# Attention with a mixture of experts on one core: sum rounds gathered, q's turn and the proposals moved within the attention steps

## The chip, the core and the metric

The kernel runs on one core of a Trainium2 chip. The time is that of one execution on the device in microseconds (us); a kernel's time is the median of several executions. The engines are TensorE (PE, with its weight loads as PEld), VectorE (DVE), ScalarE (ACT), GpSimd (POOL) and SyncE (SP, which issues DMAs).

## What is computed

Attention with a soft cap over 8 batches, 12 heads, 448 positions of 64 numbers; its output, as 3584 tokens of 768 numbers, goes through a layer of 8 experts, in which each token is given to one expert by the sorted order of all the gate logits, with at most 448 tokens per expert.

```python
scores = scale * np.matmul(q, k.transpose(0, 1, 3, 2))
scores = cap * np.tanh(scores / cap)
attn = np.exp(scores - np.max(scores, axis=-1, keepdims=True))
attn = attn / (np.sum(attn, axis=-1, keepdims=True) + 1e-09)
x = np.matmul(attn, v)            # tokens x 768
logits = x @ w_gate               # 3584 x 8
# pairs (token, expert) by falling logit; a token gets the first expert with room
h = np.maximum(x[mask] @ w1[e], 0.0); out[mask] = h @ w2[e]
```

## The kernel before, in words

The attention stage takes the first 320 us or so. `attention` (L18) walks through 24 steps g = 3b + m: a step has four heads of batch b, and a batch has a first, a second and a third step (m = 0, 1, 2). The order of the instructions of TensorE, ScalarE, VectorE and SyncE is that in which the Python code calls them; each engine works through its own row in order. Matrices lie transposed: rows are keys or features, columns are the 448 queries.

In a step, `qk(g,r)` for r = 0 to 6 is a scores group (L200): four products of 64x64 tiles into a buffer psS, of which there are two, then a tanh on ScalarE (L201) that empties the buffer into the tile e. After two or three tanh follows one exponential over them (L206). `avq(g-1,...)` multiplies the values with the exponentials of the step before (L240, into psA), `av_out` copies the result into xT on VectorE (L261). `tr(g+1,0)` and `tr(g+1,1)` turn k and q of the next step on VectorE (L180); the next step's scores need both. `esum` adds the exponentials on VectorE (L211: et in two parts, 'e1' at a step's end and 'e2' in the next, and es, two instructions, 'r').

The work on finished batches is strewn over the steps of the next ones. During batch b:

- `rnd(b-1,r)`, the sum rounds (L272): products with 32 columns of weights into one buffer psM, which give the sums of the exponentials (from es) and the gate's logits (from xT) of batch b-1. There are four rounds. For b up to 5 ("early" batches) rounds 0 and 1 are in the second step behind the fourth scores group, rounds 2 and 3 in the third step behind the second. For batch 0, round 0 has its sums twice.
- `logit(b-1)` in the third step: VectorE copies the sums out of PSUM (L280), TensorE transposes them (L286), VectorE divides and adds up the logits into L1 (L301, L303, L306).
- `xt(b-2,p)`, in early batches: TensorE transposes xT (L39), VectorE multiplies by the reciprocals into xn (L54). Pieces 0 to 3 are in the first step, 4 and 5 in the second; then xn goes to memory.
- `on_logits(b-2)`: the proposals (L519 to L547), 18 small VectorE instructions which find each token's best expert and cut its logit in pieces; r_VA (L528) is one of their results. They are in the first step, behind `xt` and ahead of `tr(g+1,1)`.
- `on_turn(b-2)`: only for b-2 = 3, thus in batch 5's second step: TensorE turns r_VA of batches 0 to 3 (L557), VectorE copies it (L555).

```python
            if m==1 and bb>=0:
                if early: rnd(bb,0); rnd(bb,1)
                else:
                    rnd(bb,2); spill(bb)
                if bb>0: on_turn(bb-1)
```

(bb is b-1.) From batch 6 on the rounds are in other places, the x pieces are put off until after the attention, and a step begins with fewer values products. After the attention, a search on VectorE and TensorE finds the limits of the first expert, and then the experts' products follow to the end.

Of the kernel before, what the change touches and what calls it, by code (L numbers as in the profile page):

```python
# [17 lines left out]
def attention(nc, tc, c1, xp, ep, nv, pM, q, k, v, cap, w_gate, xs, L1, ident, on_logits, on_turn, NDEF, xd, setup, mark):  # L18
# [42 lines left out]
    with ExitStack() as ctx:  # L61
# [10 lines left out]
        def load(g,part,lo=0,hi=HG,first=False):  # L72
            if g>=N: return
            b,m=divmod(g,NQ)
            h0=4*m
            if part==2:
                vz=nv.tile([128,7*HG*D],F32,name="nv")
                if whole(g):
                    nats[g,2]=vz.rearrange("p (r h d) -> p r h d",r=7,h=HG)
                    for o in range(2):  # L80
                        w=64*(1-o)
                        for t in range(HG): nc.sync.dma_start(nats[g,2][w:w+64,:,t,:],v[b,h0+o+2*t].rearrange("(r s) d -> s r d",s=64))
                    return
                z=vz[:,:6*HG*D].rearrange("p (j h d) -> p j h d",j=3,d=D); zh=vz[:,6*HG*D:].rearrange("p (h d) -> p h d",d=D)
                nats[g,2]=(z,zh)
                vv=v[b,h0:h0+4,0:384].rearrange("h (j p) d -> j p h d",j=3)
                for j in range(3): nc.sync.dma_start(z[:,j],vv[j])
                for o in range(2):
                    w=64*(1-o)
                    nc.sync.dma_start(zh[w:w+64],v[b,h0+o:h0+o+3:2,384:448].rearrange("t s d -> s t d"))  # L90
                return
            if lo==0: nats[g,part]=nat.tile([128,HG*NB,32],F32,name="kq"[part])
            z=nats[g,part]
            src=(k,q)[part]
            for t in range(2):
                for a in range(2):
                    w=(2*t+a)*32
                    (nc.scalar if first and a else nc.sync).dma_start(z[w:w+32,lo*NB:hi*NB,:],src[b,h0+2*t+lo:h0+2*t+hi,:,a*32:a*32+32].rearrange("h (k s) d -> s (h k) d",s=32))
# [21 lines left out]
        def gates():  # L120
            for g in range(NQ):
                for t in range(2):
                    nc.sync.dma_start(wgs[t*64:t*64+64,2*g:2*g+2,:],w_gate[(4*g+2*t)*D:(4*g+2*t+2)*D].rearrange("(m d) e -> d m e",d=D))
            for p in range(NP):
                for h in range(HG):
                    hp=slice(h*64,h*64+64); c=(16+16*pos(p))%32+8*h
                    nc.gpsimd.tensor_copy(gw[hp,p,c:c+8],wgs[hp,p,:])
            for h in range(2): nc.gpsimd.tensor_copy(wgd[h*64:h*64+64,:,h*E:h*E+E],wgs[h*64:h*64+64,NP-2:NP,:])
# [7 lines left out]
        def vload():  # L136
            b,m=divmod(N-1,NQ); h0=4*m
            z=nat.tile([128,HG*NB,32],F32,name="vq",bufs=1)
            for t in range(2):
                for a in range(2):  # L140
                    w=(2*t+a)*32
                    nc.sync.dma_start(z[w:w+32],v[b,h0+2*t:h0+2*t+2,:,a*32:a*32+32].rearrange("h (k s) d -> s (h k) d",s=32))
            vt['n']=z
# [33 lines left out]
        def tr(g,part,lo=0,hi=HG):  # L177
            if g>=N: return
            if lo==0: tks[g,part]=tp.tile([128,HG,S],F32,name="t"+"kq"[part])
            nc.vector.transpose(tks[g,part].rearrange("p m s -> p (m s)")[:,lo*S:hi*S],nats[g,part][:,lo*NB:hi*NB,:].rearrange("p k d -> p (k d)"))  # L180
        GRP=((0,1),(2,3),(4,5,6)); LOC={r:(gi,n) for gi,rs in enumerate(GRP) for n,r in enumerate(rs)}
        def ev(g,r):
            gi,n=LOC[r]
            return eh[g,gi][:,n]
        ex=lambda g,o,j: ev(g,3*o+j if g==0 else 2*j+o)
        wait=[]; G2=(B-NDEF+2)*NQ
        def qk(g,r):
            gi,n=LOC[r]
            if n==0: eh[g,gi]=ep.tile([128,len(GRP[gi]),2,S],F32,name=f"e{gi}")
            ps=pS.tile([128,2,512],F32,name="psS")  # L190
            if r<6 and not whole(g):
                o,u=divmod(r,3) if g==0 else divmod(r,2)[::-1]
                for h in range(2):
                    hp=slice(h*64,h*64+64)
                    for c in range(2): nc.tensor.matmul(ps[c*64:c*64+64,h,:S],tks[g,0][hp,o,u*128+c*64:u*128+c*64+64],tks[g,1][hp,o,:],start=True,stop=True)
            else:
                for o in range(2):
                    for h in range(2):
                        hp=slice(h*64,h*64+64); w=64*(1-o)
                        nc.tensor.matmul(ps[w:w+64,h,:S],tks[g,0][hp,o,r*64:r*64+64],tks[g,1][hp,o,:],start=True,stop=True)  # L200
            nc.scalar.activation(ev(g,r),ps[:,:,:S],AF.Tanh,scale=sr[0])  # L201
            while wait: wait.pop(0)()
            e=eh[g,gi]
            if g==N-1 and gi==2: e=ev(g,r)
            elif n<len(GRP[gi])-1: return
            act=lambda: nc.scalar.activation(e,e,AF.Exp,scale=sr[1],bias=bias)  # L206
            if gi<2 and (g>=G2 or 0<g<4): wait.append(act)
            else: act()
# [53 lines left out]
        def rnd(b,r,last=None):  # L262
            if r==0 and b not in misc: misc[b]=pM.tile([128,512],F32,name="psM")
            ps=misc[b]; last=len(R)-1 if last is None else last
            for i in range(2 if b==0 and r==0 else 1):
                for k,kind,m,n in R[r]:
                    if kind=='g':
                        if i: continue
                        lhs=gw[:,2*m+n,:]; rhs=xT[b][:,2*m+n,:]
                    elif b==0 and m==0: lhs=one0[:,i,n,:]; rhs=es_t[0][:,i,n,:]  # L270
                    else: lhs=ones[:,m,n,:]; rhs=es_t[b*NQ+m][:,n,:]
                    nc.tensor.matmul(ps[k*32:k*32+32,:S],lhs,rhs,start=r==0 and i==0,stop=r==last or (r==1 and k in (1,2)))  # L272
        lgs={}
        def spill(bb):
            if B-NDEF<=bb<B-2:
                spilled[bb]=xd[bb-(B-NDEF)]
                nc.sync.dma_start(spilled[bb],xT[bb])
        def logit_in(b):
            lgs[b]=xp.tile([128,S],F32,name="lg",bufs=1)
            nc.vector.tensor_copy(lgs[b],misc.pop(b)[:,:S])  # L280
# [49 lines left out]
        for g in range(N):  # L330
            b,m=divmod(g,NQ); bb=b-1
            for z in LD.get(g,()): load(int(z[0]),int(z[1]))
            if g>2:
                load(g+1,2); load(g+3,0); load(g+3,1)
            if g==2: gates()
            last=g==N-1
            if g==N-8: vload()
            if g==N-5: vgate()
            if g==N-3: vback()
            qk(g,0); qk(g,1)  # L340
            early=bb-1<B-NDEF; late=not early
            if early and bb>0 and m<2:
                for p in ((0,1),(4,5))[m]: xt(bb-1,p)
            if m==2 and bb>=0:
                if early:
                    for r in (2,3): rnd(bb,r)
            order=g>=G2 or 0<g<4; head=0<g<4
            for j in range(1 if head else 2 if order else 3): avq(g-1,j,0)
            if head: qk(g,2); avq(g-1,1,0)
            tr(g+1,0)  # L350
            if m==2 and bb>=0 and early:
                logit_in(bb); spill(bb)
            for w in ('e2','r'): esum(g-1,w)
            if g==N-6: vturn()
            if not head: qk(g,2)
            if order: avq(g-1,2,0)
            if m==2 and late: rnd(bb,3)
            qk(g,3)
            if order: qk(g,4)
            if m==0:  # L360
                if early and bb>0: xt(bb-1,2); xt(bb-1,3)
                if not early: rnd(bb,0); rnd(bb,1)
                if bb>0: on_logits(bb-1)
            if m==1 and bb>=0:
                if early: rnd(bb,0); rnd(bb,1)
                else:
                    rnd(bb,2); spill(bb)
                if bb>0: on_turn(bb-1)
            if m==2 and late: logit_in(bb)
            if m==2 and bb>=0 and (early or b==B-1): logit(bb)  # L370
            tr(g+1,1)
            if order: qk(g,5)
            else: qk(g,4)
            avq(g-1,0,1)
            if head: qk(g,6)
            avq(g-1,1,1)
            if not order: qk(g,5); avq(g-1,2,1)
            if not head: qk(g,6)
            if order: avq(g-1,2,1)
            avq(g-1,3,1)  # L380
            if not last: esum(g,'e1')
            if g: av_out(g-1,0); av_out(g-1,1)
            if m==2 and late and b<B-1: logit(bb)
        g=N-1; b=B-1
# [797 lines left out]
```

## Time and profile before

| | us |
|---|---|
| median of three executions | 860.55 |
| lowest and highest | 860.23, 860.87 |
| the profiled execution | 861.69 |
| its span in the trace | 859.9 |

| engine | busy us | share of the span |
|---|---|---|
| PE | 835.1 | 97% |
| DVE | 617.8 | 72% |
| ACT | 582.3 | 68% |
| POOL | 390.5 | 45% |

The busy time of PE is a modelled one, as matmuls overlap; where it stands still is better seen in the chain of waits, which goes back from the last instruction to what released it at each step. A timeline gives each engine's instructions in order of time, with the idle time ahead of one and what ended it in brackets. In the chain a piece begins where the one before it ends; "issue" is time in which nothing is seen to be waited for.

### The profile page before, as it was taken

To read this page: it belongs to the slowest core of one execution; us is meant where nothing else is said; L and a number is where in the kernel's file an instruction comes from. 1 tells how busy PE (TensorE), PEld (TensorE's weight loads), DVE (VectorE), ACT (ScalarE), POOL (GpSimd) and SP (SyncE) were. 2 spreads that over 40 slices of the span, in tenths; PEclk is the share of its full clock that TensorE was granted. 3 is DMA by queue.
4 is the path that set the end of the run, shared out by engine and by line. 5 is a ranking of instruction groups with operands and counts; after the bars stand their busy time and mean duration, and the time that the engine had idled before them with its cause. 6 is when DMAs were issued, how large, how long until landed. Compare 5 with 4: busy or idle time off the path is not lost.

```text
span 859.9 us, 16866 instructions
## 1 busy us (share of the span) xinstructions
PE 835.1 (97%) x5838; PEld 589.2 (69%) x5838; DVE 617.8 (72%) x1992; ACT 582.3 (68%) x776; POOL 390.5 (45%) x556
## 2 busy tenths in 40 slices
PE   6999999999999998899999999999999999999997
PEld 3334444444433334588888888888898889999997
DVE  5787988989897967876877987968878864263210
ACT  6998898989899887575284584575655754544421
POOL 8210000000000007675377497595677668859851
PEclk9999999999999999999999999999999999999999
DMA  8979877585986007870863896986978959959921
GB/s 145 163 122 166 180 130 151 108 173 93 218 189 125 2 2 253 253 239 0 281 204 107 238 278 208 284 250 226 262 213 238 298 161 239 309 191 295 287 74 56
DMA packets 368485, 159.28 MB, mean 185 GB/s; under 512 B 287088, under 2 KB 355312, under 8 KB 367888
## 3 DMA queue, kind: packets, MB, share of 16 engines
q1 hardware_dynamic: 357728, 128.30, 60.9%
q0 software_dynamic: 4688, 22.02, 7.6%
q10 hardware_dynamic: 5984, 7.88, 2.6%
q8 instruction: 46, 0.75, 0.4%
q14 instruction: 39, 0.32, 0.1%
HBM read 107.24 MB, written 42.66 MB: 174 GB/s over the span
## 4 chain that ended last, share of the span: by engine, by line
PE 72%; issue 7%; ACT 7%; DVE 5%; DMA 3%; SPq 3%; POOL 2%; ACTq 0%; POOLq 0%; DVEq 0%
PE psH L995 22%; PE psH L1057 18%; PE psA L240 12%; PE psS L200 12%; ACT e L201 3%; PE psM L272 3%; ACT e L206 2%; DVE cmpD L587 1%; PE psM L39 1%; POOL out_dram L1015 1%; DMA xz<-xgl 1%; DMA xg<-xz 1%; SPq L1039 1%; SPq L861 1%; SPq L939 1%
## 5 line engine op out<-in xcount | busy, mean ns | idle before, releaser
L1057 PE MATMUL psH<-hh,w2h 128*128 128x448 f32 x672 | 185.3, 367 | 0.0
L201 ACT ACTIVATE e<-psS 128x896 f32<-128x896 f32 x168 | 147.5, 910 | 26.4 <-PE psS L200 20.8
L200 PE MATMUL psS<-tq,tk 64*64 64x448 f32 x1248 | 141.1, 542 | 8.3 <-ACT e L201 7.7
L206 ACT ACTIVATE e<-e,bias 128x1792 f32<-128x1792 f32 (+2 forms) x74 | 147.3, 1992 | 1.8
L995 PE MATMUL psH<-xgh,w1h 128*128 128x448 f32 (+1 forms) x384 | 141.8, 369 | 0.1
L995 PE MATMUL psH<-xgh,w1l 128*128 128x448 f32 (+1 forms) x384 | 140.0, 365 | 0.0
L995 PE MATMUL psH<-xgl,w1h 128*128 128x448 f32 (+1 forms) x384 | 135.4, 366 | 0.0
L873 POOL TENSOR_TENSOR w2l<-w2r,w2h 128x768 fp32r<-128x768 f32 x64 | 131.1, 2052 | 9.2 <-ACT w2h L866 8.4
L873 POOL TENSOR_TENSOR w1l<-w1r,w1h 128x768 fp32r<-128x768 f32 x62 | 114.9, 1854 | 43.2 <-ACT w1h L866 43.2
L240 PE MATMUL psA<-e,nv 64*64 64x448 f32 x1232 | 134.1, 538 | 0.0
L1057 PEld LDWEIGHTS psH<-hh,w2h 128*128 128x128 f32 x672 | 124.8, 188 | 7.7
L535 POOL TENSOR_SCALAR r_Bt<-r_b 112x4 f16<-112x4 int32 x1 | 0.2, 199 | 272.4 <-DVE rin L309 272.4
L1057 PE MATMUL psH<-hh,w2l 128*128 128x448 f32 x336 | 115.2, 366 | 0.0
L200 PEld LDWEIGHTS psS<-tq,tk 64*64 64x64 f32 x1248 | 46.9, 132 | 79.2 <-issue 45.8
L240 PEld LDWEIGHTS psA<-e,nv 64*64 64x64 f32 x1232 | 49.4, 133 | 66.0 <-issue 61.9
L995 PEld LDWEIGHTS psH<-xgh,w1h 128*128 128x128 f32 x384 | 72.5, 189 | 4.8 <-ACT xgh L956 0.3
L995 PEld LDWEIGHTS psH<-xgl,w1h 128*128 128x128 f32 x384 | 72.3, 188 | 4.4 <-DVE xgl L957 0.2
L866 ACT ACTIVATE w2h<-w2r 128x768 fp32r<-128x768 f32 x64 | 75.0, 1184 | 0.5 <-DMA w2r<-in_moe_w_dram 0.5
L995 PEld LDWEIGHTS psH<-xgh,w1l 128*128 128x128 f32 x384 | 72.2, 188 | 4.4
L1004 ACT ACTIVATE hh<-psH 128x448 fp32r<-128x448 f32 x56 | 30.4, 543 | 60.4 <-PE psH L995 57.0
L1057 PEld LDWEIGHTS psH<-hh,w2l 128*128 128x128 f32 x336 | 63.2, 188 | 4.0
L898 POOL DMA_INDIRECT xg<-xs,idx x32 | 32.5, 1014 | 65.3 <-DVE zz L750 37.6
(397 smaller groups left out, 1392.8 us busy)
## 6 DMA issues: line engine op xcount, KB each, us to landing
w1r<-in_moe_w_dram SPq DMA_DIRECT2D x64, 384.0 KB, 7.1
w2r<-in_moe_w_dram SPq DMA_DIRECT2D x64, 384.0 KB, 6.4
k<-in_k_dram SPq DMA_DIRECT2D x92, 112.0 KB, 3.0
q<-in_q_dram SPq DMA_DIRECT2D x92, 112.0 KB, 3.0
nv<-in_v_dram SPq DMA_DIRECT2D x88, 112.0 KB, 3.3
yb<-yq SPq DMA_DIRECT2D x56, 168.0 KB, 5.1
on<-yb SPq DMA_DIRECT2D x7, 1152.0 KB, 7.6
xs<-xn SPq DMA_DIRECT2D x4, 1344.0 KB, 6.3
```

The lines of the kernel that those rows point to most:

```text
L39: nc.tensor.transpose(ps[:CP,j*128:(j+1)*128],xT[b][:,p,j*CP:(j+1)*CP],ident)
L200: nc.tensor.matmul(ps[w:w+64,h,:S],tks[g,0][hp,o,r*64:r*64+64],tks[g,1][hp,o,:],start=True,stop=True)
L201: nc.scalar.activation(ev(g,r),ps[:,:,:S],AF.Tanh,scale=sr[0])
L206: act=lambda: nc.scalar.activation(e,e,AF.Exp,scale=sr[1],bias=bias)
L240: for h in range(2): nc.tensor.matmul(avp[g,o][h*64:h*64+64,:S],z[w,r,h,:],ev(g,r)[w,h,:],start=r==0,stop=r==6)
L272: nc.tensor.matmul(ps[k*32:k*32+32,:S],lhs,rhs,start=r==0 and i==0,stop=r==last or (r==1 and k in (1,2)))
L866: nc.scalar.activation(view(h),r,AF.Copy)
L873: (eng or nc.gpsimd).tensor_tensor(view(l),r,view(h).bitcast(F32),op=ALU.subtract)
L898: g=nc.gpsimd.indirect_dma_start(out=row(j,n),out_offset=None,in_=xs,in_offset=bass.IndirectOffsetOnAxis(ap=res[p][0][:n,j:j+1],axis=0))
L995: nc.tensor.matmul(ps[:,o:C],a[:,c,:],b[:,c,o:],start=(m==0 and o==0),stop=(m==DC*3-1)); m+=1
L1004: nc.scalar.activation(h,ps[:,:C],AF.Relu)
L1057: nc.tensor.matmul(ps[:,:C],spl[p,2,hf,f//2][w][:,f%2,cc*128:cc*128+128],h[:,a,f],start=(m==0),stop=(m==nm-1))
```

## The change

Three things are moved within the steps, and nothing is added or taken away. For the early batches all four rounds of the sums stand in one row in the third step, behind the second scores group. `tr(g+1,1)`, q's turn, comes ahead of the second half of x's multiplications in first steps, and ahead of the logits' arithmetic in third ones. The proposals go from the first step to the second, in all batches; in batch 5 they stand directly ahead of the turn.

```diff
             if m==2 and bb>=0:
                 if early:
-                    for r in (2,3): rnd(bb,r)
+                    for r in range(4): rnd(bb,r)
...
             qk(g,3)
             if order: qk(g,4)
+            tr(g+1,1)
             if m==0:
                 if early and bb>0: xt(bb-1,2); xt(bb-1,3)
                 if not early: rnd(bb,0); rnd(bb,1)
-                if bb>0: on_logits(bb-1)
             if m==1 and bb>=0:
-                if early: rnd(bb,0); rnd(bb,1)
-                else:
+                if not early:
                     rnd(bb,2); spill(bb)
-                if bb>0: on_turn(bb-1)
+                if bb>0: on_logits(bb-1); on_turn(bb-1)
             if m==2 and late: logit_in(bb)
             if m==2 and bb>=0 and (early or b==B-1): logit(bb)
-            tr(g+1,1)
             if order: qk(g,5)
             else: qk(g,4)
```

Where this leaves the engines' rows is shown at three places of batch 5. (Line numbers behind the loop are lower by two in the changed file: L555 there is the turn, L553 its copy, L517 to L545 the proposals.) First TensorE in the second step, from its transposes to the fifth scores group, before (psS is a scores group, psA the values products, psM takes rounds, transposes and the turn):

```order
L39 MATMUL psM<-ident,xT 112x128 x8
L240 MATMUL psA<-e_2254,nv 64x448 x8
L240 MATMUL psA<-e_2301,nv 64x448 x4
L200 MATMUL psS<-tq,tk 64x448 x8
L272 MATMUL psM<-xT,gw 32x448 x2
L272 MATMUL psM<-es,ones 32x448 x2
L272 MATMUL psM<-xT,gw 32x448 x2
L272 MATMUL psM<-es,ones 32x448 x2
L557 LDWEIGHTS r_VA
L557 MATMUL psM<-r_id_372,r_VA 128x112
L200 MATMUL psS<-tq,tk 64x448 x4
```

and the end of the same stretch now, from the first values products on:

```order
L240 MATMUL psA<-e_2254,nv 64x448 x8
L240 MATMUL psA<-e_2301,nv 64x448 x4
L200 MATMUL psS<-tq,tk 64x448 x8
L555 LDWEIGHTS r_VA
L555 MATMUL psM<-r_id_372,r_VA 128x112
L200 MATMUL psS<-tq,tk 64x448 x4
L240 MATMUL psA<-e_2301,nv 64x448 x4
L240 MATMUL psA<-e_2329,nv 64x448 x4
L200 MATMUL psS<-tq,tk 64x448 x4
```

The two rounds (four rows of L272) are gone from between the fourth scores group and the turn of r_VA; the turn stands directly behind the scores groups.

TensorE at the head of the third step, before:

```order
L200 MATMUL psS<-tq,tk 64x448 x8
L272 MATMUL psM<-es,ones 32x448 x2
L272 MATMUL psM<-xT,gw 32x448 x2
L240 MATMUL psA<-e_2407,nv 64x448 x8
L240 MATMUL psA<-e_2454,nv 64x448 x4
```

and now:

```order
L200 MATMUL psS<-tq,tk 64x448 x8
L272 MATMUL psM<-xT,gw 32x448 x2
L272 MATMUL psM<-es,ones 32x448 x2
L272 MATMUL psM<-xT,gw 32x448 x2
L272 MATMUL psM<-es,ones 32x448 x4
L272 MATMUL psM<-xT,gw 32x448 x2
L240 MATMUL psA<-e_2389,nv 64x448 x8
L240 MATMUL psA<-e_2436,nv 64x448 x4
```

The rounds of the second step stand there with those of the third; x4 is the sums of rounds 1 and 2, which now adjoin.

VectorE in the second step, from the first addition of et to q's turn, before (x's multiplications are xn, r_VAt is the copy of the turn):

```order
L211 TENSOR_TENSOR et<-e_2254,e_2301 128x1792
L261 COPY xT<-psA 128x448 x2
L54 TENSOR_TENSOR xn<-psM,rin 112x4x2x64 x2
L180 STREAM_TRANSPOSE tk<-k 128x896
L211 TENSOR_TENSOR et<-et,e_2347 128x1792
L211 TENSOR_TENSOR es<-et 128x896
L211 TENSOR_TENSOR es<-es,e_2347 128x896
L555 CAST r_VAt<-psM 128x112
L180 STREAM_TRANSPOSE tq<-q 128x896
```

and now, from q's turn to r_VA:

```order
L180 STREAM_TRANSPOSE tq<-q 128x896
L517 TENSOR_REDUCE r_m<-L_70 112x4
L518 TENSOR_TENSOR r_P<-L_70,r_m 112x32
L519 TENSOR_SCALAR r_sg<-r_m 112x4
L520 TENSOR_TENSOR r_P<-r_P,r_e8m 112x32
L521 TENSOR_TENSOR r_u<-r_m,r_sg 112x4
L522 TENSOR_REDUCE r_kk<-r_P 112x4
L523 TENSOR_SCALAR r_a<-r_u 112x4
L524 TENSOR_TENSOR r_P<-r_P,r_kk 112x32
L525 SCALAR_TENSOR_TENSOR r_At<-r_a,r_op 112x4
L526 TENSOR_TENSOR r_VA<-r_P,r_At 112x32
```

The ten proposals up to r_VA (eight more follow, and then L553) stand behind q's turn of the same step, which was behind the turn's copy; before, they stood in the first step, behind x's multiplications and ahead of that step's q.

## Rows read from the trace of the kernel before

**Rows 1.** The page, part 1: busy time, share of the span, instructions of each engine
```profile
PE 835.1 (97%) x5838; PEld 589.2 (69%) x5838; DVE 617.8 (72%) x1992; ACT 582.3 (68%) x776; POOL 390.5 (45%) x556
```
**Rows 2.** Waits of PE, whole span: engine, line, waited for: total us, times, longest
```profile
PE psS L200 <- ACT e L201: 7.7, 12, 1.6
```
**Rows 3.** Chain of waits, batch 5's first to third step: start us, us, what
```profile
202.80 2.42 PE psA L240 x24
...
213.15 0.13 issue
213.28 1.73 PE psS L200 x16
...
216.03 2.60 PE psA L240 x24
...
220.14 1.64 PE psM L272 x16
221.78 0.16 PE psM L557
221.93 0.91 PE psS L200 x8
...
227.35 1.50 PE psS L200 x16
228.86 1.63 PE psM L272 x8
```
**Rows 4.** Timeline of DVE, same steps: start us, us, instruction, [idle before <- releaser]
```profile
202.40 1.29 DVE L54 TENSOR_TENSOR xn<-psM,rin 112x512 f32<-112x512 f32 x2 [0.91 <-PE psM L39]
...
209.98 0.17 DVE L519 TENSOR_REDUCE r_m<-L 112x4 f32<-112x32 f32 x1
...
211.16 0.19 DVE L528 TENSOR_TENSOR r_VA<-r_P,r_At 112x32 f16<-112x32 f16 x1
...
212.03 1.11 DVE L180 STREAM_TRANSPOSE tq<-q 128x896 f32<-128x896 f32 x1
...
216.03 1.27 DVE L54 TENSOR_TENSOR xn<-psM,rin 112x512 f32<-112x512 f32 x2
...
222.40 0.27 DVE L555 CAST r_VAt<-psM 128x112 f16<-128x112 f32 x1
...
230.53 0.62 DVE L280 COPY lg<-psM 128x448 f32<-128x448 f32 x1 [0.95 <-PE psM L272]
```
**Rows 5.** Timeline of ACT, batch 5's second step
```profile
215.86 1.70 ACT L201 ACTIVATE e<-psS 128x896 f32<-128x896 f32 x2
217.60 1.79 ACT L206 ACTIVATE e<-e,bias 128x1792 f32<-128x1792 f32 x1
```
**Rows 6.** Chain of waits, batch 1's second step and the third's start
```profile
54.18 1.50 PE psS L200 x16
...
59.44 2.39 PE psM L272 x20
...
67.25 1.50 PE psS L200 x16
```
**Rows 7.** Timeline of ACT, batch 1's second step
```profile
59.40 1.71 ACT L201 ACTIVATE e<-psS 128x896 f32<-128x896 f32 x2
```
**Rows 8.** Chain of waits, batch 6's second step
```profile
260.67 0.92 ACT e L201
...
261.63 0.98 PE psS L200 x8
```
**Rows 9.** Chain of waits, batch 7's second step
```profile
293.36 1.76 PE psA L240 x14
...
296.32 0.02 issue
```
**Rows 10.** The page, part 2: granted clock of PE in 40 slices, in tenths
```profile
PEclk9999999999999999999999999999999999999999
```

## The prediction

> **What bounds the kernel now.** I read the page's first part, the waits of TensorE, the chain of waits over the attention stage, and then the timelines of VectorE and ScalarE for the same stretch. The page says that TensorE is busy for 835.1 of 859.9 us [rows 1], and its longest wait for ScalarE anywhere is 1.6 us [rows 2]; the reader is to see that the kernel is a nearly unbroken stream of matrix products. In the chain for batch 5 [rows 3] almost every piece is a product, so a microsecond that the change takes out of the stream is won and one that it puts in is lost. The whole question is which engine comes late where the stream is re-ordered.
>
> A group of eight records (one scores group) takes 0.75 us, sixteen take 1.50 (the row at 227.35). Going into the sum rounds and out again costs something on top: sixteen records of rounds 0 and 1 fill four slots of 0.375 us, 1.50, and last 1.64; the next scores group lasts 0.91 in place of 0.75. So the two rounds cost 1.64 + 0.16 = 1.80 in the second step. Rounds 2 and 3 have only eight records, but they go in pairs and also need four slots: 1.63 (228.86).
>
> There is also a small loss at the start of each second step: an idle 0.13, scores of 1.73 in place of 1.50, values products of 2.60 where the first step has 2.42 [rows 3]. The VectorE timeline shows why: q's turn runs at 212.03, behind x's multiplications and behind the proposals that begin at 209.98, and ends only at 213.14 [rows 4]. The loss is 0.13 + 0.23 + 0.18 = 0.54.
>
> **Part 1: the second steps of batches 2 to 4.** Rounds 0 and 1 go (1.80) and the 0.54 goes, since q's turn no longer stands behind 3 us of other work. But the rounds stood between the fourth scores group and the fifth, and the fifth needs a PSUM buffer that ScalarE empties with the tanh of the third. In batch 5's frame TensorE now comes to the fifth group at 213.15 + 1.50 + 1.02 + 2.42 + 1.50 = 219.59. ScalarE works without a break before it: two tanh at 215.86, an exponential of 1.79 at 217.60 [rows 5], so the third tanh (0.92 by [rows 8]) ends at 220.31 however early TensorE is. In batch 6 the same wait shows its price: the tanh ends at 261.59, the group starts at 261.63 and lasts 0.98 [rows 8]. So TensorE waits 0.76 and loses 0.23 in the restart. The second step has 227.35 - 213.15 = 14.20 us with the turn's 0.16, thus 14.04 without it; after the change 14.04 - 1.80 - 0.54 + 0.76 + 0.23 = 12.69, 1.35 less. The third step takes the two rounds in: entry and exit are paid there already, so four more slots, +1.50. Net **+0.15 a batch, +0.45 for three**. Merging the rounds is worth 0.30 and the earlier turn 0.54, and the tanh eats both.
>
> VectorE's copy of the logits' sums in the third step already waits 0.95 for the rounds (230.53 in [rows 4]) and will wait 1.50 longer; that step grows by as much, and q's turn there now stands ahead of the logits' arithmetic, so I cost it at nothing. If that cover failed, the next step's scores would be late, as in the second steps now. SP's queue gains in the first steps: its loads of q wait for q's turns, which come earlier. The write of x's rows hangs on the second step's multiplications, which come with the transposes, 213.15 + 2.52 - 0.40 = 215.27 in place of 216.03 (0.40 as between 202.40 in [rows 4] and 202.80 in [rows 3]). POOL has nothing in the moved steps.
>
> **Part 2: batch 1.** It has no transposes, and its rounds last 2.39 us since group 0 is summed twice (six slots). Its second step runs from 54.18 to 67.25 [rows 6]. Without the rounds TensorE is at the fifth group at 59.44, but the third tanh starts at 59.40 [rows 7] and ends at 60.32. Then 0.98, and the rest of the step, 4.51 (221.93 + 0.91 to 227.35 in [rows 3]): 65.85, or 1.40 less. The third step gains six slots, 2.39 - 0.14 = 2.25. Net **+0.85**.
>
> **Part 3: batch 5's second step.** Here the turn of batches 0 to 3 (L557) stands on TensorE right behind the fourth scores group, and it reads what the proposals write. Before, these were a step old: r_VA at 211.16, the turn at 221.78, no wait. Now the proposals of batch 3 stand in the same step on VectorE, behind x's multiplications, k's turn, three sums and q's turn. TensorE comes to the turn at 219.59. VectorE: multiplications at 215.27 (above); from there to the end of the sums 222.40 - 216.03 = 6.37 [rows 4], 221.64; q's turn 1.11, 222.75; from the first proposal to r_VA 211.16 - 209.98 = 1.18 and r_VA's own 0.19: 224.12. TensorE is in-order here, so everything behind the turn stands still from 219.59 to about 224.16, 4.57 us; the fifth to seventh scores groups are queued behind it, and ScalarE waits for them. Then 0.16 + 0.91 + 4.51: the step ends at 229.74 in place of 227.35, +2.39, and with the third step's +1.50 the batch costs **+3.89**. Nothing later can take this back: the steps behind it are products again, and the search waits for the last batch.
>
> **Part 4: batches 6 and 7.** Their rounds stay. In batch 7's second step the values products start at 293.36 and the third scores group ends at 296.32, 2.96 us for 1.50 + 0.75 [rows 9], because VectorE's copies out of PSUM come late behind the proposals and q's turn. With the proposals gone from the first step I take the 2.96 - 2.25 back: **-0.66**, rounding down to leave a ScalarE hand-over. The proposals go to second steps in which VectorE has a gap; nothing waits for them there.
>
> **Sum**: 0.85 + 0.45 + 3.89 - 0.66 = +4.5 us. On the profiled execution (861.69, span 859.9) that is 866.2; it lies 1.14 above the median of the runs, so from 860.55 I forecast **865.0**.
>
> **The rivals.**
> *The clock falls in the long wait.* TensorE never stands still for more than 1.6 us before [rows 2], and the granted clock is full, 2.4 GHz, in all forty slices [rows 10]. No row shows what a stop of 4.6 us does. If TensorE came back at 1.2 GHz, the 5.58 us of the rest of that step would take up to 5.58 more; half of that, +2.8, is my value: 867.8. For it: the stop is almost three times the longest seen. Against: one stop only, and everything around it is dense. The Trainium skill, "TensorE: Matmul & The Clock Gate", section "Why this matters for your kernels", says that a TensorE left idle for long enough between bursts is put back to half its clock. By that rule this rival would be the outcome; no run here shows it.
> *The turn finds its data ready.* If VectorE came to r_VA before 219.59, by having 4.5 us less ahead of it than I count, batch 5 would cost what batches 2 to 4 cost, 0.15: 0.85 + 0.60 - 0.66 = +0.8, 861.3. Against it: the multiplications can't run before TensorE's transposes of that same step.
> *Faster: none of the new waits shows.* The place is the fifth scores group of the second steps; it decides whether the third tanh is done, and r_VA written, before TensorE is there. Then batches 2 to 5 give 1.80 + 0.54 - 1.50 = 0.84 each, batch 1 gives 2.55 - 2.25 = 0.30, batch 7 0.66: 4.3 less, 856.2. For it: TensorE bounds the kernel by the page. Against: ScalarE's row of tanh and exponential has no gap in which to be earlier.
>
> **How the numbers follow.** The forecast has 0.60, the clock 0.22, the turn in time 0.09, faster 0.05; 0.04 is for a VectorE that falls behind in the third steps too, somewhat above the forecast. The range, 863.0 to 868.2, takes the forecast with 2 us less of wait at the turn and the clock's middle value; the two cases below it hold 0.14. A run of this kernel can be told from no change at about 0.2%, 1.7 us: faster 0.05, same 0.09, slower 0.86.
>
> **What would show it.** In the changed profile TensorE should have one wait of over 4 us for r_VA in batch 5's second step, at the turn; waits of 0.7 to 0.9 us for a tanh at the fifth scores group of batches 1 to 4; one block of twenty-four records of rounds, 3.1 us, in the third steps (3.9 in batch 1); no wait for q's turn. I am wrong if the turn waits under 2 us, if second steps come out near 11.7 us, or if the whole stage after batch 5 isn't shifted by some 5 us. A granted clock under 2.4 GHz after the turn decides for the first rival.

## The result, and the profile after

The changed kernel takes 867.45 us (median of six executions, 866.97 to 867.72), the kernel before 860.82 in the same comparison (six, 860.23 to 861.43): 6.6 us slower, a ratio of 1.0077 with a 95% interval of 1.0064 to 1.0089. The forecast was 865.0 in a range of 863.0 to 868.2; the rival in which the clock falls was 867.8. The profiled execution took 867.39, with a span of 865.6.

Its page, in busy times and in the clock of the 40 slices:

```profile
PE 834.0 (96%) x5838; PEld 583.9 (67%) x5838; DVE 618.0 (71%) x1992; ACT 581.9 (67%) x776; POOL 391.9 (45%) x556
...
PEclk9999999999899999999999999999999999999999
```

Against [rows 1] almost nothing has moved: averages don't show this loss. Against [rows 10] one slice, the eleventh, has an 8.

The timeline of TensorE in the changed kernel, in batch 5's second step (start us, us, instruction, idle before it):

```profile
218.62 1.68 PE L200 MATMUL psS<-tq,tk 64*64 64x448 f32 x16
224.80 0.28 PE L555 MATMUL psM<-r_id,r_VA 112*128 112x112 f16 x1 [4.49 <-DVE r_VA L526]
```

In place of the turn without a wait at 221.78 [rows 3] there is one wait of 4.49 us for r_VA. VectorE's timeline shows why:

```profile
215.99 1.29 DVE L54 TENSOR_TENSOR xn<-psM,rin 112x512 f32<-112x512 f32 x2 [0.91 <-PE psM L39]
...
222.37 1.10 DVE L180 STREAM_TRANSPOSE tq<-q 128x896 f32<-128x896 f32 x1
...
224.55 0.19 DVE L526 TENSOR_TENSOR r_VA<-r_P,r_At 112x32 f16<-112x32 f16 x1
```

From x's multiplications to q's turn are 6.38 us, from there to the end of r_VA 2.37; the multiplications wait for TensorE's transposes of the same step, so in this order VectorE could not have been sooner.

The chain of waits goes on behind the turn (start us, us, what):

```profile
224.80 0.28 PE psM L555
225.07 1.70 PE psS L200 x8
226.78 2.99 PE psA L240 x16
229.76 0.93 PE psS L200 x8
...
232.95 1.50 PE psS L200 x16
```

The scores group takes 1.70 us where it took 0.91 [rows 3], the sixteen records of values products 2.99 where they need 1.50. The stretches of TensorE (from:to, length, busy time, granted clock, DMA share, GB/s) give the reason:

```profile
220.00:222.00 2.00, 0.31 (x4) 1.00 1.00 327
222.00:224.00 2.00, 0.00 (x0) 0.79 1.02 242
224.00:225.00 1.00, 0.20 (x1) 0.50 1.06 197
...
229.00:230.00 1.00, 1.00 (x11) 0.51 1.01 161
230.00:231.00 1.00, 1.00 (x16) 1.00 1.24 371
```

The granted clock falls from 2.4 to 1.2 GHz while TensorE stands still, and is back at 230, after 5.2 us of products at half speed. Added up over the stretches, it is low for 6.8 us.

In batch 3's second and third step the chain reads:

```profile
140.04 0.81 ACT e L201
...
140.90 0.98 PE psS L200 x8
...
146.39 1.50 PE psS L200 x16
147.89 3.14 PE psM L272 x24
```

TensorE waits 0.66 us for the third tanh (0.90 in batch 1), restarts with 0.98, and has the rounds in one block of 3.14. In batch 1 the same block takes 3.90.

A ledger of the attention, from ScalarE's exponential over three tiles (L206, 128x2688), which closes each step. The lengths run from one such start to the next:

| steps | before | after | sum |
|---|---|---|---|
| batch 1, second, third | 14.00, 13.05 | 12.58, 15.33 | +0.86 |
| batch 2, second, third | 14.09, 13.05 | 12.59, 14.57 | +0.02 |
| batch 3 | 14.04, 13.06 | 12.59, 14.56 | +0.05 |
| batch 4 | 14.05, 13.05 | 12.59, 14.57 | +0.06 |
| batch 5 | 14.20, 13.05 | 19.09, 14.56 | +6.40 |
| batch 7, second | 12.68 | 12.15 | -0.53 |

The other steps from there to the last exponential agree within 0.02. The sum, +6.86, is close to the 6.63 between the medians.

### The profile page after: what moved, and what is told of

Read it like the earlier page. It is cut to its first block, busy times and chain, and to the rows that moved or that the text cites. A ratio compares the mean times of both kernels' runs of the same rounds, so it can differ in the third digit from the quotient of the medians.

```text
span 865.6 us, 16864 instructions
## 1 busy us (share of the span) xinstructions
PE 834.0 (96%) x5838; PEld 583.9 (67%) x5838; DVE 618.0 (71%) x1992; ACT 581.9 (67%) x776; POOL 391.9 (45%) x556
## 4 chain that ended last, share of the span: by engine, by line
PE 66%; issue 10%; ACT 9%; DVE 5%; SPq 3%; DMA 3%; POOL 2%; ACTq 0%; POOLq 0%; DVEq 0%
PE psH L1055 20%; PE psH L993 19%; PE psA L240 10%; PE psS L200 10%; ACT e L201 5%; ACT e L206 3%; PE psM L272 3%; DMA xg<-xs,idx 1%; SPq L937 1%; POOL out_dram L1013 1%; PE psM L39 1%; SPq L1037 1%; SPq L859 1%; DVE cmpD L585 1%; DMA q<-in_q_dram 1%
## 5 line engine op out<-in xcount | busy, mean ns | idle before, releaser
L206 ACT ACTIVATE e<-e,bias 128x1792 f32<-128x1792 f32 (+2 forms) x74 | 147.3, 1992 | 1.8
L200 PEld LDWEIGHTS psS<-tq,tk 64*64 64x64 f32 x1248 | 44.6, 133 | 84.2 <-issue 46.0
L240 PEld LDWEIGHTS psA<-e,nv 64*64 64x64 f32 x1232 | 46.6, 134 | 68.8 <-issue 67.6
```

The lines of the kernel that those rows point to most:

```text
L240: for h in range(2): nc.tensor.matmul(avp[g,o][h*64:h*64+64,:S],z[w,r,h,:],ev(g,r)[w,h,:],start=r==0,stop=r==6)
```

## Experiments

Each run stands beside the kernel before on its own chip, whose median lay between 860.6 and 861.6; differences are taken to that one. The theory: a wait at the turn, then a lowered clock behind it; and apart from that, what the gathered rounds save is lost to a tanh. Rivals stand in each expectation.

### The turn a step later

```diff
-                if bb>0: on_logits(bb-1); on_turn(bb-1)
+                if bb>0: on_logits(bb-1)
...
             if m==2 and bb>=0 and (early or b==B-1): logit(bb)
+            if m==2 and bb>0: on_turn(bb-1)
```

> The changed kernel with only the turn of batches 0 to 3 moved, from batch 5's second step to the end of the logits in its third step, where the proposals are long done. Theory (the wait at the turn and the lowered clock behind it are the whole loss of batch 5): the second step of batch 5 falls from 19.1 to about 12.7 us, no granted clock under 1.00, and the time falls by 6.3 us from 867.45 to about 861.1, so within 0.5 us of the kernel before. Rival (VectorE is simply late from the second step on, and another instruction will wait in the turn's place): at least 864.

Measured: 861.91 against 861.64, +0.3, ratio 1.0001 (0.9992 to 1.0010): no difference to the kernel before that could be told. The chain in batch 5's second step:

```profile
220.02 0.81 ACT e L201
...
220.87 0.98 PE psS L200 x8
...
226.37 1.50 PE psS L200 x16
```

It is now as in batch 3: a tanh, 0.98, and a step of 12.58 us by ScalarE's exponentials (214.05 to 226.63). No other instruction waits in the turn's place. The whole loss of 6.4 us in batch 5 hangs on one matrix product of 0.16 us.

### The wait filled with products

Twenty, and in a second run ten, products of the identity are put ahead of the turn; nothing reads them. (Each of them shows as two records, so twenty are x40.)

```diff
         ps=s.psum()
+        for _ in range(20 if h==0 else 0): nc.tensor.matmul(ps[:,:128],s.ident,s.ident,start=True,stop=True)
         s.flip(ps,0,n,h)
```

> The changed kernel with 20 products of the identity with itself put ahead of the turn into the turn's own PSUM tile (the turn then overwrites it; nothing reads them). They fill about 4.3 of the 4.49 us in which TensorE waits for r_VA; the wait for r_VA stays as it is. Theory (the stop lowers TensorE's clock): the granted clock stays at 1.00, the fifth scores group lasts 0.9 instead of 1.70 and the values products behind it 1.5 instead of 2.99, and the time falls by the clock's share alone, 2.4 us, to 865.0. Rival (what stands behind the turn is slow for another reason, a late operand or ScalarE): the rows stay at 1.70 and 2.99 and the time at 867.4.

Measured: 866.50 against 861.64, +4.9, ratio 1.0052 (1.0038 to 1.0065). The chain, and then the stretch behind the turn (here with the busy times of all engines ahead of the clock):

```profile
220.12 4.66 PE psM L552 x40
224.78 0.05 PE psM L556
224.83 0.91 PE psS L200 x8
225.75 1.50 PE psA L240 x16
...
230.25 1.50 PE psS L200 x16
```

```profile
225.00:230.00 5.00, 5.00 (x56) 1.99 (x52) 2.43 (x6) 2.27 (x3) 0.00 (x0) 1.00 0.90 143
```

The turn comes as late as in the changed kernel (224.78 and 224.80), but the products behind it go at full speed, and the step ends 2.70 us earlier (230.25 and 232.95). From one of ScalarE's exponentials to the next the step takes 16.58 us in place of 19.09, 2.51 less; it began 0.19 earlier, and the products run on for some 0.2 us after r_VA is written. So the slow rows behind the turn are the clock's, and the clock fell because TensorE stood still, not because of what came after. By the medians the gain is smaller than by the steps: +4.9 against the changed kernel's +6.6 is 1.8, where the expectation had 2.4.

> As the run with 20 products, but with 10, so that TensorE stands still for about 2.3 us ahead of the turn. If the lowered clock comes from the length of the stop, a stop between the 1.64 us that the kernel before shows at full clock and the 4.49 us that lowered it: 865.0 if 2.3 us is short enough, 867.4 if not. I lean to 865.0. If the clock had nothing to do with the stop, 867.4.

Measured: 866.95 against 861.64, +5.3, ratio 1.0056 (1.0042 to 1.0070), with executions from 865.8 to 868.0. TensorE's timeline and the stretch around the turn:

```profile
224.65 0.22 PE L556 MATMUL psM<-r_id,r_VA 112*128 112x112 f16 x1 [2.06 <-DVE r_VA L526]
224.81 0.98 PE L200 MATMUL psS<-tq,tk 64*64 64x448 f32 x8
```

```profile
220.00:225.00 5.00, 2.94 (x29) 2.60 (x29) 4.86 (x19) 3.37 (x3) 0.00 (x0) 1.00 1.01 262
```

A stop of 2.06 us left the clock at 1.00, as I leaned to; the step takes 16.57 us. The mean granted clock of the four executions without a profile is 0.998 to 1.000, where those of the changed kernel have 0.995 to 0.997. The total doesn't show it alone: in the profiled execution, the slowest of the five, the gather of the first expert's rows landed late, long after the attention, and TensorE, with little to do between 366.9 and 370, lost its clock there (timeline, then stretches of TensorE):

```profile
368.25 0.44 PE L903 MATMUL psX<-ident,xg 128*128 128x128 f32 x2 [1.36 <-DMA xg<-xs,idx]
...
369.66 0.69 PE L903 MATMUL psX<-ident,xg 128*128 128x128 f32 x2 [0.65 <-DMA xg<-xs,idx]
```

```profile
369.00:370.00 1.00, 0.35 (x3) 0.79 0.06 25
370.00:371.00 1.00, 1.00 (x5) 0.50 0.03 12
```

Both were compared with the changed kernel only across chips. Therefore the changed kernel and the one with twenty products ran once more on one chip.

> The changed kernel as it is, beside the next run on one chip, since the share of the clock was so far read between two chips. Theory: 6.6 us above before; in the profile the granted clock is 0.50 for the rest of batch 5's second step, as in its first profile. Rival (the lowered clock was an accident of one execution): a clock of 1.00 there and 4.2 to 4.9 us above before.

> The changed kernel with 20 products of the identity ahead of the turn, as before, now on the same chip as the changed kernel. By the chains of the two profiles, from the turn to the end of the step 5.47 in place of 8.15 us: 2.4 to 2.7 us below the changed kernel. If the clock's share were the 1.8 us that the medians of the two chips show, 1.8 below.

Measured: 866.65 (866.17 to 867.58) for the changed kernel and 865.38 (865.05 to 865.82) for the filled one, against 860.65: +6.0 and +4.7, ratios 1.0068 (1.0054 to 1.0082) and 1.0055 (1.0042 to 1.0069). In the profile of the first the clock is at 0.50 in the same place:

```profile
224.00:226.00 2.00, 1.24 (x9) 0.50 0.86 150
```

But the medians are only 1.3 apart, less than either number that I gave; the last exponentials of the two profiles stand 2.63 apart (310.61 and 307.98), 2.51 if one counts from batch 1's first step. The mean clock of the executions gives one reason: over the eleven of the changed kernel it lies between 0.995 and 0.997, and 0.997 goes with 866.2 to 867.4 us, 0.995 and 0.996 with 867.4 to 867.7, so the faster ones were low for a shorter time. The 6.8 us of the profiled ones, both at 0.996, make 0.996 by themselves (1 - 0.5 x 6.8 / 865.6), and the six executions at 0.997 must have had less. The rest of the kernel varies as well: from the last exponential to the end the twelve profiles take from 554.7 to 558.3 us. Whether the two are all of the difference stays open. The clock's share is 2.5 us in the profiles and 1.3 to 1.8 between medians.

### The rounds alone

```diff
-                    for r in (2,3): rnd(bb,r)
+                    for r in range(4): rnd(bb,r)
...
-                if early: rnd(bb,0); rnd(bb,1)
-                else:
+                if not early:
                     rnd(bb,2); spill(bb)
```

> The kernel before with only the four rounds of the early batches gathered in the third step; q's turn and the proposals stay where they were, so the turn of batches 0 to 3 finds its data ready. Theory (what gathering saves, 0.30 a batch, is lost again in a wait for the third tanh at the fifth scores group of the second step): batch 1 costs 0.86, batches 2 to 5 between 0.05 and 0.15 each, together 1.1 to 1.5 over the 860.8 of before, 862.1; the second steps of batches 2 to 5 last 12.6 to 12.7 us, the third steps 14.55. Rival (the gathering is a gain and the loss is elsewhere): 0.30 less for each of five batches, 859.3.

Measured: 863.19 against 861.64, +1.6, ratio 1.0018 (1.0009 to 1.0027), just above the 1.1 to 1.5 of the expectation. Gathering the rounds is a loss by itself. The chain in batch 3's second step:

```profile
133.93 0.12 issue
134.06 1.74 PE psS L200 x16
...
136.81 2.60 PE psA L240 x24
139.41 0.81 PE psS L200 x5
...
140.25 0.93 ACT e L201
...
141.22 0.98 PE psS L200 x8
```

The tanh bounds it here too. The second step comes to 12.78 us (134.20 to 146.98 by ScalarE's exponentials) and the third to 14.57: 0.25 more than before, where I gave 0.05 to 0.15. The late q's turn is still there (0.12 and 1.74), so the third scores group ends late, at 140.23, and the tanh begins behind it instead of behind ScalarE's own work.

### q's turn alone

```diff
             if order: qk(g,4)
+            tr(g+1,1)
             if m==0:
...
-            tr(g+1,1)
             if order: qk(g,5)
```

> The kernel before with only q's turn moved ahead of the second half of x's multiplications; rounds and proposals stay. Theory (the loss of 0.54 at the start of the second steps comes from the proposals, which hold up not only q's turn but also the copies out of PSUM that free the buffers of the values products): the scores start in time, but the values products then wait for the copies, so a second step gains 0.1 at most and the time is 0.1 to 0.6 us below before. Rival (q's turn was what was late): 0.36 to 0.54 for each of four second steps, 1.4 to 2.2 us below before.

Measured: 860.36 against 860.59, -0.2, ratio 0.9999 (0.9990 to 1.0008), inside the first theory's 0.1 to 0.6. In the chain of batch 5's second step

```profile
212.73 1.50 PE psS L200 x16
...
215.25 2.59 PE psA L240 x22
217.84 0.22 PE psS L200 x2
```

the scores start in time and last 1.50, not 1.73, but the values products stretch until the copies of VectorE have freed their buffer, as its timeline shows, with two copies that end at 215.68, and the waits of TensorE's weight loads between 214 and 219 (engine, line, waited for: total us, times, longest):

```profile
214.53 1.15 DVE L261 COPY xT<-psA 128x448 f32<-128x448 f32 x2
...
PEld psA L240 <- DVE xT L261: 0.5, 2, 0.3
```

This wait takes back what the scores gained: the second steps of batches 2 to 5 are as long as before, within 0.01 us.

### The proposals alone, and with q's turn

```diff
-                if bb>0: on_logits(bb-1)
             if m==1 and bb>=0:
...
-                if bb>0: on_turn(bb-1)
+                if bb>0: on_logits(bb-1)
...
             if m==2 and bb>=0 and (early or b==B-1): logit(bb)
+            if m==2 and bb>0: on_turn(bb-1)
```

> The kernel before with only the proposals moved, from the first to the second steps, and the turn of batches 0 to 3 moved to the end of the logits in batch 5's third step, so that it never waits; rounds and q's turn stay. Theory: the second steps of batches 2 to 5 lose their 0.54 (14.04 to 13.5 us), batch 7 gains 0.53 as in the changed kernel: 2.7 us below before, ratio 0.9969. Rival (q's turn of the second step, now behind the proposals, comes late for the third step, or ScalarE bounds the shorter step): less than 1 us below before.

Measured: 857.49 against 860.59, -3.1, ratio 0.9965 (0.9951 to 0.9978). The chain in batch 5's second step has neither loss:

```profile
210.95 1.50 PE psS L200 x16
...
213.47 2.42 PE psA L240 x24
```

> As the run with the proposals and the turn moved, and q's turn ahead of x's multiplications as well; only the rounds stay as before. This is the changed kernel less its two losses (the gathered rounds and the turn that waits). Theory: 2.7 us below before, the same as with the proposals alone within 0.3 us, and the version to keep. Rival (q's turn adds a gain of its own): over 0.5 us below the run without it.

Measured: 857.80 against 860.59, -2.8, ratio 0.9966 (0.9952 to 0.9979): no different from the proposals alone. Both beat the kernel before and the changed one.

### The proposals with the turn right behind them

```diff
-                if bb>0: on_logits(bb-1)
             if m==1 and bb>=0:
...
-                if bb>0: on_turn(bb-1)
+                if bb>0: on_logits(bb-1); on_turn(bb-1)
```

> The kernel before with only the proposals moved to the second steps; the turn stays in batch 5's second step, directly behind them, and the rounds and q's turn stay as before. So the turn waits here as well, but from 1.5 us later on (two rounds stand before it) and for data that come 1.1 us earlier (q's turn is behind the proposals). Theory: TensorE waits some 1.8 us for r_VA at the turn with the clock at 1.00 before and after, and the time is 2.7 - 1.8 = 0.9 us below before. Rival (any wait at the turn lowers the clock): about 1.5 us above before.

Measured: 860.16 against 860.59, -0.4, ratio 0.9999 (0.9990 to 1.0008). The timeline of TensorE at the turn, and the stretch:

```profile
221.05 0.22 PE L556 MATMUL psM<-r_id,r_VA 112*128 112x112 f16 x1 [1.86 <-DVE r_VA L527]
```

```profile
220.00:225.00 5.00, 3.95 (x41) 1.68 (x45) 4.83 (x20) 2.20 (x3) 0.00 (x0) 1.00 0.94 183
```

The wait is the 1.8 us of the expectation and the clock stays full in this profile. It need not have in every execution: two of the eleven have a mean clock of 0.996 and 0.997, lower than any of the 21 of the kernel before on this chip (0.998 to 1.000), and take 861.21 and 861.80 us. Where the clock fell in them no profile shows. At the last exponential of the attention, counted from the end of batch 1's first step, the gain is 0.8 us; of that the medians show a half, and the interval takes in both.

## Why the prediction was right or wrong

**The direction and the place were right, the forecast value was 2.4 us too low.** The turn's wait was worked out as 4.57 us from VectorE's rows and is 4.49; the second step without it as 12.69 and is 12.59, as TensorE waits 0.66 for the tanh in place of 0.76; batch 1 as +0.85 and is +0.86; batches 2 to 4 as +0.15 each and are +0.02 to +0.06; batch 7 as -0.66 and is -0.53. The third steps grew by 1.51 for 1.50. That the VectorE copies and q's turn of the third steps cost nothing held: the first steps behind them are unchanged. The other two rivals, a turn that finds its data ready and a gain without new waits, fall with the wait of 4.49 us and the waits for the tanh.

**The term that was mis-sized is part 3, batch 5: +3.89, measured +6.40.** Its last line, "0.16 + 0.91 + 4.51", took the rest of the step at full speed. In the trace this rest, from the turn to the next step, takes 8.15 us (224.80 to 232.95) in place of 5.58, 2.57 more, because the clock fell in the stop. This was the first rival, with 0.22, priced at +2.8 and at 867.8, where 867.45 came out. So the forecast without the clock was given 0.60 and the rival that happened 0.22. The longest stop of the kernel before, 1.6 us [rows 2], said nothing on one of 4.5, and I held "one stop only" against it; the fall needs no more than one. The run with the filled wait is what the forecast described: +4.7 and +4.9 in the two comparisons, against the +4.5 of the sum, and a second step of 16.58 us, where the prediction had 2.39 more than 14.20, 16.59.

That 867.45 lies in the range is no merit of the sum: the range was drawn to take in the rival's value. And that value came close by luck. Half of the 5.58 us was taken without a row on how long the clock stays low; in the trace it was low for 5.2 us of products, which costs about half of that, and then rose. The other parts came out 0.18 us below the sum together.

The Trainium skill, "TensorE: Matmul & The Clock Gate", section "Why this matters for your kernels", says that long idle gaps between bursts put TensorE back to half its clock. By that rule the trace agrees, with 0.50 granted behind the stop of 4.49 us. It does not cover the fall in the run with ten products, at stops of 1.36 and 0.65 us.

**What the parts are worth** was argued ahead and is now shown by single runs: the rounds alone cost 1.6 where the separate blocks looked like 0.30 a batch to be saved; q's turn alone gives nothing that could be told (-0.2, inside the interval); the proposals alone give 3.1, provided that the turn waits for the next step. I had put the 0.54 of each second step down to q's turn being late. The run with q's turn alone shows that this was half a reason: the copies that free the values' buffers stand behind the proposals as well, and as long as they do, an earlier q gains nothing. With the proposals gone, the second steps of batches 2 to 5 take 13.51 us, and the earlier q adds nothing to that. So the changed kernel had one good move in it, worth 3.1 us, and lost that gain and 6.6 us more.

## What to carry to other kernels

Before an instruction is moved next to the one that feeds it, look on which engine it makes the others queue: a product of 0.16 us that waits in an in-order row stops everything behind it, and a step's delay for it cost nothing that could be told (+0.3). A block taken out of a saturated engine is only a gain where no other engine's chain ends at that place; here the rounds were what hid the third tanh. And a long stop on TensorE has two prices, its length and the clock afterwards: when a sum has such a stop, the lowered clock belongs in the forecast itself.

## What the runs showed of the hardware

A single stop of 4.49 us in a stream that was otherwise dense lowered the granted clock to 0.50, in both profiles of the changed kernel, while stops of 1.86 and 2.06 us at the same place left it at 1.00 in the one profile of each. The longest stop of the kernel before, 1.6 us, left it there too. The length of one stop isn't all, though: in the run with ten products, stops of 1.36 and 0.65 us with a few transposes between them lowered it at the first expert's gather, where the profiles of the kernel before and of the changed one kept it. At the low level a scores group took 1.70 us instead of 0.91 and sixteen records of values products 2.99 instead of 1.50, about twice as long, and TensorE had worked without a gap since 224.80 before the clock rose again at 230. How long it is low differs between executions of one kernel: the mean clock of the changed one is 0.995 to 0.997.
